# Three raw-word buffers instead of two, and one throw-away buffer instead of two, in a fused attention and mixer kernel

## The chip, the cores and the metric

One core of one Trainium2 chip runs the kernel. The metric is the device time of one execution in microseconds; of several executions the median counts. TensorE is called PE here, VectorE DVE, ScalarE ACT, GpSimd POOL, and SyncE, which issues nearly all DMAs, SP.

## What is computed

Causal attention over 4 batches, 12 heads, 448 tokens and 64 columns a head; then a mixer block (token mixing 448 to 256 to 448, channel mixing 768 to 1536 to 768); then a second block with a rotation of its input. Cut to what matters:

```python
attn = softmax(where(causal, q @ k.T / 8, -1e9)); x = attn @ v      # (4, 448, 768)
h   = relu(x.T @ w_tok1) @ w_tok2;  u = x + h.T
x2  = u + relu(u @ w_ch1) @ w_ch2
th  = x2 @ w_theta
y   = w_tok_r @ (x2 * cos(th)) + w_tok_i @ (x2 * sin(th));  u2 = x2 + y
out = u2 + relu(u2 @ w_ch)
```

The weights come as 64-bit floats, so that each weight is two 32-bit words in memory, and the kernel makes its own numbers of them.

## The kernel before

**Stages.** The first stage does attention in 24 pairs of heads, seven tiles of scores a pair, so 168 steps (the loop over `steps`, lines 600 to 643). A step makes one tile of scores on PE, its mask and minimum on DVE (L338), its exponential on ACT (L340), and four steps later the product with v. Pairs 0 to 11 turn the exponentials on PE (L347); later pairs send them through a DMA transpose issued on SP (L363). Beside the steps, channel-mixing units of the first block (`ch1_unit`, `ch2_unit`, matmul lines 227 to 229) are strewn in from step 50 on; each needs a weight tile `ws` that SP loads back from memory (`stream_tile`, L222). After the steps come the rest of these units and the second block.

**The rounding pipeline.** Twenty-eight weight tiles are made during the first stage: tiles 0 to 3 are the token weights (512 or 448 columns), tiles 4 to 27 the channel weights (768 columns). `ROUNDINGS` gives each tile j its step `at_step`: 3, 4, 8, 9 and then 14, 17, 20, 24 and so on to 92. A tile goes through this chain:

- `fetch(j)` takes a `raw` buffer and loads the 64-bit words on SP (L170),
- `round_first(j)` at `at_step`: ACT reads the high words (`abs64`, L173) into a `wf` tile,
- `round_bits(j)` one step later: three DVE instructions (L180, L181, L182), of which the last two read `raw`; after L182 the buffer is free. For a channel tile, ACT then squares the tile into a throw-away tile `junk`, of which only the sum is used (`squares`, L124),
- `round_split(j)` and `round_store(j)` three and five steps later make two half-precision parts and store them (L536).

Two steps after `at_step` the next fetch is put in: before the change `fetch(j + 2)`, into the buffer that tile j has just left.

**Six late tiles** (the weight of the last matmul, `convert_late` and `convert`) use the same `raw` and `wf` buffers. Their fetches are tied behind the load of q of pair 16 on SP (`loads[16]`, line 543).

**What sets the order.** The kernel is written as one list; a planner that runs its own model of the chip (`schedule_with_timeline_sim=True`) puts the instructions of each engine into a fixed order, and places a buffer's next user by when the model sees the buffer free. At run time each engine, and SP's queue too, goes through its list in order: an instruction that waits holds up all that stands behind it.

Of the kernel before, what the change touches and what calls it, by code (L numbers as in the profile page):

```python
# [25 lines left out]
FH = 6  # L26
NEG = -1.0e30
PSC = 32768.0
BUFS = dict(ut=12, h2=8, acc=12, ws=8, wf=3, raw=2, sb=3, ph=3, pt=5, t=3, junk=2)
NATIVE = {0, 1, 2, 3, 4, 5, 6, 7}  # L30
NATPV = {0, 1, 2, 3, 4, 5, 6, 7, 8, 9, 10, 11}
AHEAD, LAG, LOOK = 500, 4, 2
# [22 lines left out]
def fused(ctx, tc, q, k, v, w_tok1, w_tok2, w_ch1, w_ch2, w_theta, w_tok, w_ch, out):  # L55
# [53 lines left out]
    def hl_tile(tag):  # L109
        return main.tile([P, 2, S], F16, tag=tag, name=tag, bufs=BUFS[tag])  # L110

# [8 lines left out]
    def squares(dst, src):  # L120

        j = main.tile([P, E], BF16, tag="junk", name="junk", bufs=BUFS["junk"])
        with nc.allow_low_precision(reason="it only chooses a power of two"):
# [25 lines left out]
    def acc_tile():  # L149
        return main.tile([P, S], F32, tag="acc", name="acc", bufs=BUFS["acc"])  # L150

# [14 lines left out]
    def raw_tile():  # L166
        return cv.tile([P, E, 2], U32, tag="raw", name="raw", bufs=BUFS["raw"])

    def fetch64(src, raw):
        nc.sync.dma_start(out=raw[:, :src.shape[-1]].rearrange("p n w -> p (n w)"), in_=src.bitcast(U32))  # L170
# [13 lines left out]
    def wf_tile():  # L184
        return main.tile([P, E], F32, tag="wf", name="wf", bufs=BUFS["wf"])

# [23 lines left out]
    def ws_tile():  # L210
        return main.tile([P, 2, E], F16, tag="ws", name="ws", bufs=BUFS["ws"])

# [34 lines left out]
    for j in range(BUFS["sb"]):  # L247
        sb = ac.tile([P, 512], F32, tag=f"sb{j}", name=f"sb{j}")
# [4 lines left out]
    def tok_weights(n):  # L253
        if n < 2:
            cols = slice(n * 512, (n + 1) * 512)
            return w_tok1[:, cols], wt1[:, :, cols]
        return w_tok2[:, (n - 2) * S:(n - 1) * S], wt2[:, n - 2]
# [177 lines left out]
    h2 = {}  # L435
# [51 lines left out]
    def load_unit(n):  # L487
        if n < len(units) and n not in loaded and (n >= 24 or n in stored):
            b, fh, c, t = units[n]
            loaded[n] = stream_tile(wd[f"c{c}", fh, t])  # L490
# [4 lines left out]
    def split_ready():  # L495

        b = halves[0]
        if b < B and None not in accs[b]:
            s = s_u[:, b:b + 1]
            power(p_u[:, b:b + 1], s, sq_u[b])  # L500
            for d in range(DT):
                uTs[b][d] = hl_tile("ut")
                split_to(pick("uhi"), uTs[b][d], accs[b][d], s)
            halves[0] += 1

    def fetch(j):
        if j < len(ROUNDINGS):
            n = ROUNDINGS[j][1]
            src = tok_weights(n + 4)[0] if n < 0 else jobs[n][0]
            fetched[j] = src, raw_tile()  # L510
            fetch64(*fetched[j])

    def round_first(j):
        src, raw = fetched[j]
        rounding[j] = wf_tile()[:, 0:src.shape[-1]]
        abs64(rounding[j], raw)

    def round_bits(j):
        n, f = ROUNDINGS[j][1], rounding[j]
        round64(f, fetched.pop(j)[1])  # L520
        if n < 0:
            split_w(tok_weights(n + 4)[1], rounding.pop(j))
        else:
            rounding[j] = f, row_squares(f)

    def round_split(j):
        n = ROUNDINGS[j][1]
        if n >= 0:
            f, sq = rounding.pop(j)
            rounding[j] = ws_tile()  # L530
            split_scaled("P", rounding[j], f, jobs[n][2], sq)

    def round_store(j):
        n = ROUNDINGS[j][1]
        if n >= 0:
            nc.sync.dma_start(out=jobs[n][1], in_=rounding.pop(j))  # L536
            stored.add(n)
# [3 lines left out]
    def convert_late(n):  # L541
        while made[0] < min(n, len(late)):
            with tc.issue_after(loads[min(LATE_CONVERT, max(loads))].ins):
                convert(*late[made[0]])
            made[0] += 1
# [4 lines left out]
    def run_units(n):  # L550
        for _ in range(n):
            u = at[0]
            load_unit(u)
            b, fh, c, t = units[u]
            if c == 1 and t == 0:
                h_scale[0] = domain(b, fh)
            if c == 1:
                ch1_unit(b, uTs[b], fh, t, loaded[u])
            else:
                ch2_unit(b, uTs[b], accs[b], fh, t, loaded[u])  # L560
            loaded[u] = None
            at[0] += 1
            for ahead in range(LOOK + (u >= 24)):
                load_unit(at[0] + ahead)
            if at[0] % 24 == 2 and 1 <= at[0] // 24 <= 3:
                x_scale(at[0] // 24 - 1)
# [16 lines left out]
    def late_step(n):  # L583
        b, pr, t = steps[n]
        pp = pairs[b, pr]
        pv(pp, *TILES[t])
        if mixes:
            with tc.issue_after(pp.pv.ins):
                mix_tokens()
        if t == 6:  # L590
            if pr % 2 == 0:
                xgs[b, pr // 2] = [ap2.tile([P, 4, 2 * P], F32R, tag=f"xg{z}", name=f"xg{z}", bufs=1) for z in range(2)]
            finish(pp, xbufs[pr % 2], xgs[b, pr // 2])
            if pr % 2 == 1:
                mixes.append((b, pr // 2))

    def queued(pp):
        return tc.issue_after(pp.sent.ins) if pp.sent is not None else ExitStack()

    for n, (b, pr, t) in enumerate(steps):  # L600
        if t == 0:
            eng.update(ENGINES.get(b * NPR + pr, {}))
        if t == 0:
            pairs[b, pr] = Pair(b, pr, parts[b, pr])
        with tc.high_priority(AHEAD):
            scores(pairs[b, pr], *TILES[t])
        if n == 0:
            fetch(0)
            fetch(1)
        for j, (at_step, _) in enumerate(ROUNDINGS):  # L610
            if at_step == n - ROUND_BITS:
                with tc.issue_after(pairs[b, pr].first.ins):
                    round_bits(j)
            if at_step == n:
                with tc.issue_after(pairs[b, pr].last.ins):
                    round_first(j)
            if at_step == n - ROUND_FETCH:
                with queued(pairs[b, pr]):
                    fetch(j + 2)
            if at_step == n - ROUND_STORE:  # L620
                with queued(pairs[b, pr]):
                    round_store(j)
        if n >= 140:
            convert_late((n - 136) // 4)
        if t == 0 and (b, pr) != (B - 1, NPR - 1):
            nx = (b + (pr + 1) // NPR, (pr + 1) % NPR)
            with tc.high_priority(AHEAD), ExitStack() as es:
                if nx == (0, 1):
                    es.enter_context(tc.issue_after(loads[0].ins))
                parts[nx] = prep(*nx)  # L630
        if n >= LAG:
            with tc.high_priority(AHEAD):
                late_step(n - LAG)
            with tc.issue_after(pairs[steps[n - LAG][0:2]].pv.ins):
                for j, (at_step, _) in enumerate(ROUNDINGS):
                    if at_step == n - ROUND_SPLIT:
                        round_split(j)
                if n in (b2 * 42 + 48 for b2 in range(B)):
                    split_ready()
        if n == FIRST_UNIT - 4:  # L640
            load_unit(0)
            load_unit(1)
        run_units(sum(at_step == n for at_step in UNIT_STEPS))
# [169 lines left out]
    for b in range(B):  # L813
        raw, x2 = raws[b], x2s[b]
# [138 lines left out]
```

## Time and profile before

| | us |
|---|---|
| median of 3 runs | 913.49 (911.87 to 916.33) |
| the profiled execution, its own time | 915.05 |
| its span, first to last instruction | 913.3 |
| PE busy in the span | 871.4 (95%) |
| DVE busy | 630.5 (69%) |
| ACT busy | 537.2 (59%) |
| mean granted clock of PE | 0.98 of full speed |

The rows further down come from that one execution. Times in them are microseconds from the start of the span. A busy PE isn't PE at its peak, since matmuls are pipelined; what is read here are the stretches in which PE is idle, what ended them, and the granted clock in and after them.

### The profile page before, as it was taken

How to read it: one execution, taken by the hardware profiler on the slowest of the kernel's cores; microseconds unless marked ns; L12 is line 12 of the kernel's file. 1: busy time of each engine (PE TensorE's matmuls, PEld its weight loads, DVE VectorE, ACT ScalarE, POOL GpSimd, SP SyncE). 2: the span in 40 equal slices, each digit the busy share in tenths (PEclk: the TensorE clock that was granted, in tenths of full speed). 3: DMA queues.
4: the chain of work that ended last, by engine and by line, in shares of the span. 5: the costliest groups of instructions: out<-in, count | busy, mean ns of one | idle time of the engine just before them, and what ended most of it. 6: DMA issues, size and time to landing. Idle time of an engine off the chain costs nothing.

```text
span 913.3 us, 16742 instructions
## 1 busy us (share of the span) xinstructions
PE 871.4 (95%) x5979; PEld 566.4 (62%) x5979; DVE 630.5 (69%) x1499; ACT 537.2 (59%) x1247; POOL 169.6 (19%) x313
## 2 busy tenths in 40 slices
PE   7899899998879989999999999999999999999998
PEld 6778767776746656666665664556545556555554
DVE  6888897969998564748686337867875556666442
ACT  6777786767656553627574328546755456566441
POOL 2233243314121010011201103152111001001000
PEclk9999999999889989999999999999999999999999
DMA  6665776757699974849467469740450231331011
GB/s 174 205 207 170 278 245 222 265 192 213 165 284 290 292 169 120 193 140 204 120 181 219 142 186 299 277 140 10 135 151 18 96 113 37 94 113 35 23 63 71
DMA packets 105795, 149.67 MB, mean 164 GB/s; under 512 B 61104, under 2 KB 72304, under 8 KB 105712
## 3 DMA queue, kind: packets, MB, share of 16 engines
q1 hardware_dynamic: 105168, 147.59, 54.4%
q0 software_dynamic: 384, 0.79, 0.4%
q8 instruction: 47, 0.77, 0.4%
q14 instruction: 36, 0.29, 0.1%
q10 hardware_dynamic: 160, 0.23, 0.1%
HBM read 112.39 MB, written 22.81 MB: 148 GB/s over the span
## 4 chain that ended last, share of the span: by engine, by line
PE 73%; DMA 13%; DVE 7%; ACT 4%; issue 2%; SPq 1%; POOL 0%; ACTq 0%; DVEq 0%; POOLq 0%
PE ps_mm L227 16%; PE ps_mm L228 16%; PE ps_mm L229 16%; DMA pt<-ph 6%; PE ps_pv L375 3%; PE ps_sc L227 3%; PE ps_sc L331 3%; PE ps_sc L228 3%; PE ps_sc L229 3%; DMA ws<-w_c 2%; DMA raw<-in_w_ch_dram 2%; PE ps_pv L386 2%; PE ps_mm L347 2%; PE ps_sc L333 1%; DMA rawt<-x2d 1%
## 5 line engine op out<-in xcount | busy, mean ns | idle before, releaser
L227 PE MATMUL ps_mm<-h,ws 128*128 128x448 f16 x432 | 152.6, 354 | 1.1 <-DMA ws<-w_c 0.6
L228 PE MATMUL ps_mm<-h,ws 128*128 128x448 f16 x432 | 152.8, 354 | 0.0
L229 PE MATMUL ps_mm<-h,ws 128*128 128x448 f16 x432 | 152.6, 354 | 0.0
L227 PEld LDWEIGHTS <-ws 128*128 128x128 f16 x720 | 70.8, 98 | 69.0 <-issue 5.6
L229 PEld LDWEIGHTS <-ws 128*128 128x128 f16 x720 | 70.8, 98 | 64.5 <-issue 4.2
L228 PEld LDWEIGHTS <-ws 128*128 128x128 f16 x720 | 70.8, 98 | 61.6 <-issue 4.4
L340 ACT ACTIVATE sb<-sb,mx 128x320 f32<-128x320 f32 (+3 forms) x168 | 89.3, 532 | 32.0 <-DVE mx L338 30.8
L227 PE MATMUL ps_mm<-ut,ws 128*128 128x448 f16 x288 | 102.4, 357 | 5.5 <-DMA ws<-w_c 3.7
L228 PE MATMUL ps_mm<-ut,ws 128*128 128x448 f16 x288 | 102.8, 357 | 0.4 <-DVE ut L193 0.3
L229 PE MATMUL ps_mm<-ut,ws 128*128 128x448 f16 x288 | 102.7, 357 | 0.0
L338 DVE CUSTOM_DVE_ANT_0 sb<-ps_sc,mask 128x320 f32<-128x320 f32 (+3 forms) x168 | 74.3, 454 | 16.5 <-PE ps_mm L347 13.3
L124 ACT ACTIVATE junk<-acc 128x448 bf16<-128x448 f32 x72 | 41.1, 571 | 60.7 <-DVE acc L845 42.8
L375 PE MATMUL ps_pv<-v_raw,ptf 128*128 128x128 f32 (+1 forms) x456 | 65.9, 284 | 0.6 <-ACT sb L340 0.4
L375 PEld LDWEIGHTS ps_pv<-v_raw,ptf 128*128 128x128 f32 x456 | 61.7, 200 | 5.6 <-issue 1.9
L160 POOL TENSOR_SCALAR h<-t 128x448 f16<-128x448 f32 x48 | 33.1, 692 | 144.6 <-ACT t L459 144.3
L360 DVE SCALAR_TENSOR_TENSOR ph<-sb,ph 128x64 f16<-128x64 f32 (+3 forms) x156 | 44.3, 327 | 22.0 <-ACT ph L157 21.6
L459 ACT ACTIVATE t<-ps_mm,c_scale 128x448 f32<-128x448 f32 x48 | 29.9, 625 | 49.9 <-PE ps_mm L229 41.4
L157 ACT ACTIVATE ph<-sb 128x192 f16<-128x192 f32 (+3 forms) x84 | 36.0, 441 | 37.4 <-DMA pt<-ph 36.8
L461 DVE TENSOR_TENSOR h<-t,h 128x448 f16<-128x448 f32 x48 | 31.0, 649 | 32.3 <-POOL h L160 32.2
L130 POOL TENSOR_SCALAR f<-p_w,c_h 128x1 f32<-128x1 f32 x48 | 22.9, 479 | 145.1 <-DVE acc L473 129.0
L331 PE MATMUL ps_sc<-kh,qs 128*128 128x256 f32 (+2 forms) x112 | 44.6, 407 | 4.4 <-DVE g L140 2.3
L331 PE MATMUL ps_sc<-k_pad,q_raw 128*128 128x192 f32 (+3 forms) x112 | 41.1, 467 | 8.0 <-DMA k_pad<-in_k_dram 4.4
(210 smaller groups left out, 2115.4 us busy)
## 6 DMA issues: line engine op xcount, KB each, us to landing
ws<-w_c SPq DMA_DIRECT2D x120, 384.0 KB, 4.2
raw<-in_w_ch_dram SPq DMA_DIRECT2D x30, 768.0 KB, 4.6
w_c<-ws SPq DMA_DIRECT2D x30, 384.0 KB, 3.4
q_raw<-in_q_dram SPq DMA_DIRECT2D x16, 448.0 KB, 3.9
k_raw<-in_k_dram SPq DMA_DIRECT2D x16, 448.0 KB, 5.1
v_raw<-in_v_dram SPq DMA_DIRECT2D x24, 288.0 KB, 3.6
x2d<-acc SPq DMA_DIRECT2D x24, 224.0 KB, 2.9
acc<-x2d SPq DMA_DIRECT2D x24, 224.0 KB, 2.9
```

Source lines behind the costliest of these rows:

```text
L124: nc.scalar.activation(j[:, 0:src.shape[-1]], src, AF.Square, accum_out=dst)
L157: nc.scalar.activation(dst, src, AF.Copy, scale=scale)
L160: e.tensor_scalar(out=dst, in0=src, scalar1=scale, scalar2=0.0, op0=ALU.mult, op1=ALU.add)
L227: nc.tensor.matmul(ps, lhsT=ka(a[:, 0]), rhs=kb(b[:, 0]), start=first, stop=False)
L228: nc.tensor.matmul(ps, lhsT=ka(a[:, 0]), rhs=kb(b[:, 1]), start=False, stop=False)
L229: return nc.tensor.matmul(ps, lhsT=ka(a[:, 1]), rhs=kb(b[:, 0]), start=False, stop=last)
L331: nc.tensor.matmul(ps[:, 0:n], lhsT=lhs, rhs=cut(pp.kh), start=True, stop=pp.kl is None)
L338: pp.first = nc.vector.tensor_tensor_reduce(out=dst, in0=src, in1=msk, op0=ALU.add, op1=ALU.min, scale=-0.125, scalar=3.0e38, accum_out=pp ...
L340: pp.last = nc.scalar.activation(sb[:, 0:kk], sb[:, 0:kk], AF.Exp, bias=pp.mx[:, j:j + 1], scale=-1.0, accum_out=pp.sm[:, j:j + 1])
L360: nc.vector.scalar_tensor_tensor(out=dst, in0=sb[:, c0:c1], scalar=PSC, in1=hi[:, c0:c1], op0=ALU.mult, op1=ALU.subtract)
L375: pp.pv = nc.tensor.matmul(pp.ps[:, reg:reg + n], lhsT=pt[:, u], rhs=pp.v[0][:, vt * D:vt * D + n], start=(u == 0), stop=(u == len(blks) - 1))
L461: gates[0] = nc.vector.tensor_tensor(out=t[:, 1], in0=f, in1=t[:, 0], op=ALU.subtract)
```

## The change

The `raw` tag gets three buffers instead of two (6 KiB more in each partition: 768 columns of two 4-byte words), the `junk` tag one instead of two (1.5 KiB less: 768 columns of 2 bytes). The three places where a fetch is put in follow the buffer count: three fetches at the first step instead of two, and later `fetch(j + 3)` where `fetch(j + 2)` stood. Nothing else is touched.

```diff
-BUFS = dict(ut=12, h2=8, acc=12, ws=8, wf=3, raw=2, sb=3, ph=3, pt=5, t=3, junk=2)
+BUFS = dict(ut=12, h2=8, acc=12, ws=8, wf=3, raw=3, sb=3, ph=3, pt=5, t=3, junk=1)
@@ -605,8 +605,8 @@
         if n == 0:
-            fetch(0)
-            fetch(1)
+            for j in range(BUFS["raw"]):
+                fetch(j)
@@ -616,7 +616,7 @@
             if at_step == n - ROUND_FETCH:
                 with queued(pairs[b, pr]):
-                    fetch(j + 2)
+                    fetch(j + BUFS["raw"])
```

## Rows read from the trace of the kernel before

**Rows 1.** Windows by stage: stretch, length, busy us (instructions) per engine, PE clock, DMA, GB/s.

```profile
0.00:120.00 120.00, 106.91 (x697) 91.17 (x698) 94.66 (x264) 88.44 (x239) 39.31 (x67) 0.96 0.65 208
120.00:220.00 100.00, 99.50 (x686) 76.09 (x686) 84.50 (x201) 72.68 (x177) 31.62 (x42) 1.00 0.66 228
220.00:340.00 120.00, 103.10 (x895) 69.51 (x894) 98.32 (x262) 73.92 (x185) 19.79 (x36) 0.90 0.92 237
...
540.00:914.00 374.00, 365.66 (x2104) 204.13 (x2102) 231.56 (x454) 205.26 (x410) 53.81 (x112) 1.00 0.33 107
```

**Rows 2.** ACT's timeline: start, us, line, operation, and in brackets the idle before it.

```profile
17.54 0.62 ACT L173 ACTIVATE wf<-raw 128x448 f32<-128x448 f32 x1 [1.07 <-DMA raw<-in_w_tok_dram]
...
28.98 0.89 ACT L173 ACTIVATE wf<-raw 128x768 f32<-128x768 f32 x1 [2.21 <-DMA raw<-in_w_ch_dram]
...
64.68 0.90 ACT L173 ACTIVATE wf<-raw 128x768 f32<-128x768 f32 x1 [2.46 <-DMA raw<-in_w_ch_dram]
...
95.70 0.90 ACT L173 ACTIVATE wf<-raw 128x768 f32<-128x768 f32 x1 [2.20 <-DMA raw<-in_w_ch_dram]
```

**Rows 3.** PE's timeline: the matmuls that ended PE's idle time beside those four.

```profile
19.73 1.02 PE L331 MATMUL ps_sc<-k_pad,q_raw 128*128 128x448 f32 x2 [1.03 <-DVE mx L338]
...
30.79 1.86 PE L331 MATMUL ps_sc<-k_pad,q_raw 128*128 128x448 f32 x2 [2.13 <-DVE mx L338]
...
66.18 0.55 PE L347 MATMUL ps_mm<-ident,sb 128*128 128x128 f32 x3 [1.49 <-ACT sb L340]
...
97.20 0.55 PE L347 MATMUL ps_mm<-ident,sb 128*128 128x128 f32 x3 [1.34 <-ACT sb L340]
```

**Rows 4.** Windows of PE alone: stretch, length, busy us, clock, DMA share, GB/s.

```profile
30.00:36.00 6.00, 5.21 (x24) 0.72 0.39 124
68.00:72.00 4.00, 4.00 (x22) 0.57 0.77 230
98.00:104.00 6.00, 5.71 (x36) 0.72 0.63 236
...
256.00:264.00 8.00, 4.25 (x16) 0.57 1.12 259
```

**Rows 5.** SP's timeline: when DMAs were issued (a row may join two).

```profile
11.79 0.47 SPq L277 DMA_DIRECT2D k_pad<-in_k_dram  x1
...
13.42 3.62 SPq L170 DMA_DIRECT2D raw<-in_w_tok_dram  x2
...
22.25 0.33 SPq L170 DMA_DIRECT2D raw<-in_w_ch_dram  x1
...
59.48 0.33 SPq L170 DMA_DIRECT2D raw<-in_w_ch_dram  x1
```

**Rows 6.** DVE's timeline: the last reader of raw tile 1 and of raw tile 6.

```profile
15.94 0.68 DVE L182 SCALAR_TENSOR_TENSOR wf<-raw,wf 128x512 uint32<-128x512 uint32 x1
...
44.82 0.95 DVE L182 SCALAR_TENSOR_TENSOR wf<-raw,wf 128x768 uint32<-128x768 uint32 x1
```

**Rows 7.** A DMA issue on the page: count, KB each, median us from issue to landing.

```profile
ws<-w_c SPq DMA_DIRECT2D x120, 384.0 KB, 4.2
```

**Rows 8.** SP's own waits: for whom, us in total, times, longest us.

```profile
SPq L170 <- DVE wf L182: 67.9, 24, 6.7
```

**Rows 9.** SP's timeline: first and last fetches of the six late tiles.

```profile
248.38 1.47 SPq L170 DMA_DIRECT2D raw<-in_w_ch_dram  x2
...
456.15 0.33 SPq L170 DMA_DIRECT2D raw<-in_w_ch_dram  x1
```

**Rows 10.** The chain that ended last, at the weight tile behind the late fetches.

```profile
250.37 9.64 DMA ws<-w_c
```

**Rows 11.** PE's timeline: the matmul that waited for that weight tile.

```profile
260.06 0.55 PE L227 MATMUL ps_mm<-ut,ws 128*128 128x448 f16 x1 [3.75 <-DMA ws<-w_c]
```

**Rows 12.** The view of tile junk: the sum's read-out (ns min/median/max), longest idle before writers.

```profile
L124 ACT ACTIVATION_READ_ACCUMULATOR junk<-acc x72: 187/189/203, 50.4 to 883.0; 128x1 bf16 x72
...
  DVE acc L845: 42.8, 19
```

## The prediction

> **What bounds the kernel now.** I read the windows by stage first [rows 1]. From 540 us on PE is busy for 365.66 of 374 us (the rest is mostly the end), and from 120 to 220 us for 99.50 of 100, both at clock 1.00: there PE sets the pace and no buffer of raw words buys anything. PE is idle in two stretches: 13.1 us of the first 120 us (120 - 106.91), at clock 0.96, and 16.9 us from 220 to 340 us, at clock 0.90. Raw words are fetched in both, so I looked at each for itself.
>
> In the first stretch ACT's timeline shows four instructions that waited for a raw tile to land, 1.07 + 2.21 + 2.46 + 2.20 = 7.94 us [rows 2]; there are no others of any length among the 34 tiles. All four are the first reader, L173. ACT takes its list in order, so exponentials that were ready stood behind that wait, and PE ran dry beside each of them: 1.03 + 2.13 + 1.49 + 1.34 = 5.99 us idle [rows 3]. The reader is to see two things there: PE isn't waiting for the weights (no matmul of that stretch needs them yet), and what ended the idle time is named as ACT's L340 or DVE's L338, which themselves stood behind L173. After the second, third and fourth of these gaps the granted clock is at its lower level (1.2 instead of 2.4 GHz) for some microseconds; averaged over the rows' windows it is 0.72, 0.57 and 0.72 [rows 4]. What PE lost by that is its busy time times what was missing: 5.21 x 0.28 + 4.00 x 0.43 + 5.71 x 0.28 = 1.46 + 1.72 + 1.60 = 4.78 us. The gap at 19.73 us shows no such fall.
>
> **The third buffer, tiles 0 to 27.** A fetch can't start before the buffer it wants has been read for the last time, which is L182. With two buffers, the fetch of tile 4 left at 22.25 us and that of tile 9 at 59.48 us [rows 5]; each left as tile j - 2 was done, and landed when ACT was already waiting. With three it waits for tile j - 3: for tile 4 that is tile 1, done at 15.94 + 0.68 = 16.62 us, for tile 9 it is tile 6, done at 44.82 + 0.95 = 45.77 us [rows 6]. So they can leave 5.6 and 13.7 us earlier, against ACT waits of 2.21 and 2.46 us. Tile 2, which left at 13.42 us [rows 5], is fetched at the start and has about eight microseconds more, against 1.07 us; tile 13 is like tile 9. All four waits are covered, the tightest with 5.6 - 2.2 = 3.4 us to spare. What goes: the idle time, 5.99 us, and the slow clock behind it, 4.78 us, together 10.8 us. The low end is the idle time alone, 6.0 us, if PE's clock falls anyway because other small gaps stand nearby. I take 10.8, since the three windows of slow clock follow right behind three of the gaps and end within some microseconds. Whether the saving lasts to the end of the kernel: what follows is a stage in which PE has no room [rows 1], so a head start there is kept, and all later work is tied to steps and not to a time.
>
> **What the earlier fetches move past.** On SP the fetch still stands two steps behind its tile's start and still waits for the same L182; what is in the transfer is another tile. So the time that SP stands still for this (67.9 us in 24 waits [rows 8]) and what waits behind it, the loads of q, k and v, stay as they are: no cost. One transfer is new at its place: tile 2 (448 KB) at the start, behind tiles 0 and 1. The next DMA in SP's queue left at 11.79 us [rows 5]. If the new transfer were still running then, it would cost at most about the landing time of a load of its size, 4.2 us [rows 7], on the load of pair 2, which has no reader at once; I take zero and keep no more than that in the range. The last place, where tile 27 was fetched, falls empty.
>
> **The late tiles.** The six late tiles share the buffers. Their fetches are tied behind q of pair 16, and right behind it two of them left at 248.38 us, both buffers being free; the last went only at 456.15 us [rows 9]. The weight tile `ws` that was issued next took 9.64 us to land [rows 10], where 4.2 us are usual [rows 7], and PE stood idle for 3.75 us until it came [rows 11], with 2.25 us of another gap just before. So the two late tiles ahead of it cost that load 9.64 - 4.2 = 5.4 us, 2.7 us each. With three buffers free, a third late fetch will most likely go at the same place: another 2.7 us, and PE waits for all of it, since it had nothing else in its order. The ends are 0 (the third comes behind `ws`) and 2.7 us; below nothing too, a gain of 2.7 us, if the planner puts one late fetch less ahead of `ws` than now. I take 2.7. The last late fetch no longer goes at 456 us, where nobody waited for it: nothing.
>
> The Trainium skill, DMA: Bandwidth & Descriptors, sections "Queues, rings and completion order" and "Issuing engines are not separate DMA queues", speaks against this part of the change: a ring's descriptors are taken in the order in which they were put in, and all issuers share the same 16 DMA engines, so a deep prefetch holds up whatever is behind it. By that rule, carried to its end, every further raw tile ahead of a load that somebody waits for costs its whole transfer. The trace agrees at this one place (9.64 against 4.2 us); it does not in the first 105 us, where no load beside the raw tiles was waited for once the first scores had begun. Its result as a whole is the slower rival below.
>
> **One throw-away buffer.** Every `junk` tile is written by ACT alone and read by nobody. With two buffers already every third square overwrote the first one's tile, so all but two of 115 show what a reuse costs: the longest idle time before them was for DVE's `acc` [rows 12], and none was for ACT itself. Zero. If the planner did put a wait between two squares, it would be for the sum's read-out, 0.19 us each [rows 12], which ACT at 59% busy hides, and of which only the dozen and a half in the first 105 us could reach PE: under 3.4 us, and only if each fell on a full list.
>
> **The sum.** -10.8 + 2.7 = -8.1 us. From the profiled execution, 915.05 us (span 913.3 and 1.75 around it), that is 907.0. This execution lay 1.56 us above the median of the three runs, so against the median, 913.49, it is 905.4 us.
>
> **The rivals.**
>
> *The clock falls anyway, or other small waits move in.* Then only the idle time goes: -6.0 + 2.7 = -3.3, 910.2 us. For it: in the same 120 us ACT and DVE are busy 88.44 and 94.66 us [rows 1], so they have not much room. Against it: PE resumed 0.6 to 1.6 us after each of the four L173 had ended [rows 2, 3]. 15%.
>
> *The fetches don't come earlier.* The planner may leave a fetch on SP behind a load or store that itself waits, so that it lands when it did; the time stays at 913.5, or 916.2 with the late tile's 2.7. Against it: 5.6 and 13.7 us is a lot of room to lose. 10%.
>
> *The late tiles clog the DMAs: slower.* From 220 to 340 us the DMA engines are 0.92 busy [rows 1]. The sixth late tile comes into that stage instead of at 456 us, and each bunch of late fetches goes ahead of weight tiles and transposes that PE waits for. The price of one such gap as the trace has it is 2.25 + 3.75 us idle and 4.25 x 0.43 = 1.83 us of slow clock [rows 4, 11], 7.8 us. If the two bunches (three fetches each) each cost one gap more than now, 15.6 us, and the front gives its low end, the sum is +9.6, 923.1 us. It begins to decide where the extra gaps exceed 10.8 us. For it: the 9.64 us landing. Against it: between 260 and 340 us most late fetches ran with no PE wait behind them. 10%.
>
> *The late fetches leave their place.* The order of all engines is planned anew; if `ws` then comes ahead of one raw tile more than now, the time is 913.5 - 10.8 - 2.7 = 900.0 us. 7%.
>
> **How the numbers follow.** The forecast has 58% and its own range is 902.7 (front gain whole, no late cost) to 910.2 us. The range to hold 8 in 10 takes in the rivals on either side but the slower one: 900.0 to 915.0 us. About 0.5%, 4.6 us, is what a measurement of this kernel can tell from no change. Faster by more: 58 + 7 = 65%. Within: 15 + 10 = 25%. Slower: 10%.
>
> **What would show it.** Right: no ACT wait for a raw tile at L173 in the first 110 us; PE idle in the first 120 us down from 13.1 to about 7 us and its clock there up from 0.96 to near 1.00; the turn into the next stage some 10 us earlier; three fetches in a row behind q of pair 16 and the `ws` behind them landing in 11 to 13 us. Wrong: the four waits gone but PE's idle time in the first 120 us unchanged (then ACT's wait wasn't the last one), or PE's idle time from 220 to 340 us grown by more than 5 us, or a squaring on ACT that waits for ACT.

## The result and the profile after

The changed kernel takes 905.74 us (median of 5 runs, 904.31 to 907.62) against 915.07 for the kernel before beside it (911.87 to 916.33): a ratio of 0.9903 [0.9877, 0.9929], some 9 us, where 8.1 were forecast. The execution profiled after took 907.62 us, with a span of 905.8 (913.3 before).

Windows by stage of the kernel after; columns and the lines of before are those of [rows 1]:

```profile
0.00:120.00 120.00, 104.34 (x705) 87.88 (x706) 104.69 (x276) 94.90 (x252) 37.03 (x68) 0.96 0.74 241
...
220.00:340.00 120.00, 109.72 (x940) 74.17 (x938) 99.15 (x267) 74.11 (x184) 24.96 (x36) 0.93 0.92 251
```

The first stage is a surprise: PE is idle for 15.7 us of the first 120 (13.1 before) at the same clock, 0.96, though this is where the change was to act. The stage from 220 us has what is missing: PE idle 10.3 us from 220 to 340 us instead of 16.9.

The waits for raw tiles are gone all the same. What ended ACT's idle time before L173 in the first 120 us, us and times; before, four raw tiles ended 7.94 us of it [rows 2]:

```profile
  DVE ws L193: 1.2, 2
  DMA raw<-in_w_tok_dram: 0.4, 1
```

SP's timeline after, fetches and what was issued around them ([rows 5, 9] answer to it):

```profile
4.33 1.38 SPq L170 DMA_DIRECT2D raw<-in_w_tok_dram  x3
...
16.71 0.33 SPq L170 DMA_DIRECT2D raw<-in_w_ch_dram  x1
...
40.55 0.33 SPq L170 DMA_DIRECT2D raw<-in_w_ch_dram  x1
...
240.80 0.37 SPq L279 DMA_DIRECT2D q_raw<-in_q_dram  x1
241.22 0.42 SPq L170 DMA_DIRECT2D raw<-in_w_ch_dram  x1
241.73 0.38 SPq L281 DMA_DIRECT2D k_raw<-in_k_dram  x1
242.17 0.93 SPq L170 DMA_DIRECT2D raw<-in_w_ch_dram  x2
244.87 1.67 SPq L363 DMA_TRANSPOSE pt<-ph  x1
246.59 0.58 SPq L222 DMA_DIRECT2D ws<-w_c  x1
...
295.47 0.60 SPq L170 DMA_DIRECT2D raw<-in_w_ch_dram  x1
```

Tile 4 leaves at 16.71 us (22.25 before; the prediction had 16.62) and tile 9 at 40.55 (59.48 before; 45.77 in the prediction, which left out that the front itself runs ahead).

Totals by the clock on the wall mix work that has moved, so the two traces were laid beside each other by step: when the mask of the same score tile (L338) starts. DVE's timeline, the 49th and the 55th score tile, before:

```profile
100.53 0.62 DVE L338 CUSTOM_DVE_ANT_0 sb<-ps_sc,mask 128x448 f32<-128x448 f32 x1
...
120.45 0.61 DVE L338 CUSTOM_DVE_ANT_0 sb<-ps_sc,mask 128x448 f32<-128x448 f32 x1
```

and after:

```profile
90.23 0.61 DVE L338 CUSTOM_DVE_ANT_0 sb<-ps_sc,mask 128x448 f32<-128x448 f32 x1
...
117.29 0.61 DVE L338 CUSTOM_DVE_ANT_0 sb<-ps_sc,mask 128x448 f32<-128x448 f32 x1
```

At step 48 the kernel after leads by 10.3 us, six steps later by 3.2. Worked out in the same way from one profiled execution of each kernel, in us against the kernel before (minus is earlier):

| kernel | raw, junk buffers | step 48 | 54 | 84 | 132 | 162 |
|---|---|---|---|---|---|---|
| before, start of the step | 2, 2 | 100.5 | 120.4 | 211.6 | 367.9 | 478.1 |
| after | 3, 1 | -10.3 | -3.2 | -1.2 | -10.9 | -8.0 |
| E1 | 3, 2 | -8.7 | -9.1 | -9.1 | -10.7 | -9.7 |
| E2 | 2, 1 | -6.2 | +1.3 | +3.7 | -5.3 | -4.7 |
| E3 | 3, 1 | -9.8 | -2.7 | -1.9 | -11.7 | -13.0 |
| E4 | 3, 1 | -9.3 | -2.1 | -1.1 | -11.6 | -13.9 |
| E5 | 3, 1 | -9.8 | -7.0 | -5.6 | -13.0 | -13.7 |
| E6 | 3, 2 | -8.8 | -9.8 | -9.8 | -13.3 | -10.1 |
| E7 | 3, 1 | -10.1 | -3.8 | -1.0 | -12.7 | -9.3 |
| E8 | 3, 2 | -7.5 | -8.0 | -7.4 | -15.5 | -14.0 |
| E9 | 2, 2 | -1.2 | -2.3 | -2.3 | -6.9 | -7.1 |
| E10 | 3, 2 | -7.6 | -8.2 | -7.5 | -9.6 | -11.3 |
| E11 | 2, 2 | -3.2 | -4.3 | -3.6 | -9.9 | -11.6 |

How far one execution stands for its kernel shows in pairs of kernels with nearly the same lists. On PE, ACT, DVE, POOL and SP, E9 has the lists of the kernel before up to 249 us, and yet leads by 2.3 us at step 84. E3 has those of the kernel after but for the place of one fetch at about 212 us, and is 5.0 us away from it at step 162. Differences up to that size can't be told from chance, in the front and behind it.

So in the kernel after the lead is won before step 48, all but lost until step 84 (-10.3 to -1.2, that is 9.1 us), and found again by step 132. What it is won by shows in PE alone from the start to step 48, of the kernel before, the kernel after and E2, which has two raw buffers:

```profile
0.00:100.53 100.53, 88.82 (x572) 0.96 0.64 198
0.00:90.23 90.23, 83.34 (x577) 1.00 0.72 224
0.00:94.30 94.30, 84.03 (x577) 1.00 0.67 207
```

From before to after, PE's idle time falls from 11.7 to 6.9 us, by 4.8, and the clock's part, 88.82 x 0.04 = 3.6 us, goes; together these are 8.4 of the 10.3 us.

Where it is lost: PE's timeline after, the matmuls that ended its longer idle times (in brackets the idle time and what ended it); the third row belongs to the late tiles:

```profile
108.06 0.91 PE L375 MATMUL ps_pv<-v_raw,ptf 128*128 128x64 f32 x6 [1.66 <-DVE x L398]
114.57 0.53 PE L227 MATMUL ps_mm<-ut,ws 128*128 128x448 f16 x1 [5.61 <-ACT ut L157]
...
253.98 0.23 PE L386 MATMUL ps_pv<-v_raw,pt 128*128 128x64 bf16 x1 [3.35 <-DMA pt<-ph]
```

and PE alone in windows behind that gap (stretch, length, busy us, clock, DMA share, GB/s):

```profile
114.00:117.00 3.00, 2.15 (x8) 0.50 0.94 327
117.00:120.00 3.00, 3.00 (x9) 0.50 0.87 344
120.00:123.00 3.00, 3.00 (x23) 0.89 0.02 8
```

That is 1.66 + 5.61 = 7.27 us idle, and 2.15 x 0.50 + 3.00 x 0.50 + 3.00 x 0.11 = 2.9 us of clock: 10.2 us in one place. The kernel before has no idle time over 0.7 us between steps 48 and 54. The matmul at 114.57 is the first of the first channel-mixing unit and needs `ut`, which ACT makes with the scale `s_u`. POOL makes that scale, among other small products (L130). POOL's timeline before:

```profile
115.53 0.19 POOL L130 TENSOR_SCALAR p_u<-g 128x1 f32<-128x1 f32 x1
115.68 0.99 POOL L130 TENSOR_SCALAR s_u<-g 128x1 f32<-128x1 f32 x1
116.77 0.27 POOL L130 TENSOR_SCALAR c_h<-p_fh,p_u 128x1 f32<-128x1 f32 x1
117.13 1.33 POOL L130 TENSOR_SCALAR f<-p_w,c_h 128x1 f32<-128x1 f32 x4
```

and after:

```profile
109.06 0.83 POOL L130 TENSOR_SCALAR p_u<-g 128x1 f32<-128x1 f32 x1 [5.38 <-DVE g L140]
109.99 1.17 POOL L130 TENSOR_SCALAR c_h<-p_fh,p_u 128x1 f32<-128x1 f32 x1
111.26 2.40 POOL L130 TENSOR_SCALAR f<-p_w,c_h 128x1 f32<-128x1 f32 x4
113.64 0.18 POOL L130 TENSOR_SCALAR s_u<-g 128x1 f32<-128x1 f32 x1
```

The order is another: `s_u`, for which ACT and PE wait, now stands behind `c_h` and four `f`, which the matmul at 114.57 does not need. Nothing in the diff names these instructions.

### The profile page after: what moved, and what is told of

It is laid out like the page before. It is cut to its first block, busy times and chain, and to the rows that moved or that the text cites. A ratio compares the mean times of both kernels' runs of the same rounds, so it can differ in the third digit from the quotient of the medians.

```text
span 905.8 us, 16756 instructions
## 1 busy us (share of the span) xinstructions
PE 868.4 (96%) x5979; PEld 563.7 (62%) x5979; DVE 632.0 (70%) x1499; ACT 538.1 (59%) x1247; POOL 166.0 (18%) x313
## 4 chain that ended last, share of the span: by engine, by line
PE 74%; DVE 10%; DMA 8%; ACT 3%; issue 3%; POOL 1%; SPq 1%; DVEq 0%; ACTq 0%; POOLq 0%
PE ps_mm L228 17%; PE ps_mm L227 17%; PE ps_mm L229 17%; DMA pt<-ph 4%; PE ps_sc L229 3%; PE ps_sc L227 3%; PE ps_sc L228 3%; PE ps_pv L375 3%; PE ps_sc L331 2%; PE ps_pv L386 2%; PE ps_mm L347 2%; DVE sb L338 1%; PE ps_sc L333 1%; DVE wf L181 1%; DMA ws<-w_c 1%
## 5 line engine op out<-in xcount | busy, mean ns | idle before, releaser
L338 DVE CUSTOM_DVE_ANT_0 sb<-ps_sc,mask 128x320 f32<-128x320 f32 (+3 forms) x168 | 73.8, 454 | 13.2 <-PE ps_mm L347 8.8
L375 PE MATMUL ps_pv<-v_raw,ptf 128*128 128x128 f32 (+1 forms) x456 | 63.2, 276 | 1.9 <-DVE x L398 1.7
L375 PEld LDWEIGHTS ps_pv<-v_raw,ptf 128*128 128x128 f32 x456 | 58.8, 191 | 6.9 <-ACT sb L340 1.9
L130 POOL TENSOR_SCALAR f<-p_w,c_h 128x1 f32<-128x1 f32 x48 | 24.6, 516 | 145.2 <-DVE acc L473 129.0
L473 DVE SCALAR_TENSOR_TENSOR acc<-ps_mm,f,acc 128x448 f32<-128x448 f32 x48 | 32.4, 678 | 25.1 <-PE ps_mm L229 24.9
L227 PE MATMUL ps_sc<-th,ut 128*128 128x384 f16 x144 | 46.9, 326 | 0.0
```

The lines of the kernel that those rows point to most:

```text
L227: nc.tensor.matmul(ps, lhsT=ka(a[:, 0]), rhs=kb(b[:, 0]), start=first, stop=False)
L338: pp.first = nc.vector.tensor_tensor_reduce(out=dst, in0=src, in1=msk, op0=ALU.add, op1=ALU.min, scale=-0.125, scalar=3.0e38, accum_out=pp ...
L375: pp.pv = nc.tensor.matmul(pp.ps[:, reg:reg + n], lhsT=pt[:, u], rhs=pp.v[0][:, vt * D:vt * D + n], start=(u == 0), stop=(u == len(blks) - 1))
L473: nc.vector.scalar_tensor_tensor(out=acc[d], in0=ps[:, 0:S], scalar=f, in1=acc[d], op0=ALU.mult, op1=ALU.add)
```

## The experiments

Each was timed in 5 rounds against the kernel before on its own chip: 913.95 us there for E1 to E4 (23 runs), 913.83 for E5 to E8 (14), 914.43 for E9 to E11 (17). The edits of E1 to E8 are against the kernel after, or as stated.

**E1: three raw buffers, two throw-away buffers.**

```diff
-raw=3, ... junk=1
+raw=3, ... junk=2
```

> The raw edit alone: three raw buffers, three fetches ahead, still two throw-away buffers. If the third raw buffer makes the gain: no ACT wait for raw words in the first 110 us, the step-48 scores some 10 us earlier than before, and 904 to 908 us. If the time comes from the new order that the planner happens to lay out after 200 us: the front is the same, but the end lies anywhere between 902 and 915 us, away from 905.7 by more than 2 us.

905.07 us, 0.9894 [0.9854, 0.9933]. The room of the second throw-away buffer wasn't needed: the kernel fits with both. The first window of E1:

```profile
0.00:120.00 120.00, 111.06 (x752) 92.11 (x753) 103.78 (x280) 96.03 (x257) 39.75 (x68) 1.00 0.74 236
```

This is the profile that was forecast for the change: PE idle 8.9 us (120 - 111.06), clock 1.00, the lead kept from step 48 (8.7) to step 84 (9.1). POOL makes `s_u` right behind `p_u`, as before, and PE has no long gap there. So with the raw buffers alone the front's gain is there and stays, and what takes it back in the kernel after comes with the throw-away buffer. The total doesn't show it: E1 can't be told from the kernel after.

**E2: one throw-away buffer alone**, with the two raw buffers and the fetches of before. Against the kernel before:

```diff
-raw=2, ... junk=2
+raw=2, ... junk=1
```

> The throw-away edit alone: one junk buffer, two raw buffers. If junk costs nothing and brings nothing: 913 to 916 us, the four ACT waits for raw words (7.9 us) and PE's idle time from 220 to 340 us (16.9 us) as before. If what moved the late part is the planner's order, and one buffer less is enough to change that order: more than 3 us away from before on either side, with the four waits still there.

912.19 us, 0.9972 [0.9944, 0.9999]. PE's timeline of E2 at the first unit:

```profile
118.33 0.53 PE L227 MATMUL ps_mm<-ut,ws 128*128 128x448 f16 x1 [4.83 <-ACT ut L157]
```

The same gap without the third raw buffer, and the same loss: from -6.2 to +3.7, that is 9.9 us between steps 48 and 84 (9.1 in the kernel after). With E1 this is shown from both sides, and it holds in all thirteen kernels: between steps 48 and 54 the six with one throw-away buffer have an idle time of 2.5 to 5.6 us at the first unit, and the seven with two have none over 0.7 us anywhere there. E2 also has more lead at step 48 than it should have: ACT's waits for channel tiles fell from three to two (4.1 us) in its new order, and PE's clock did not fall before step 48 (1.00 against 0.96), though ACT still waits for raw tiles. From 211 to 368 us it wins 9.0 us back, and so ends near no change, 1.8 us below the kernel before, outside both of the ranges that were expected. PE is idle for 12.0 us from 220 to 340 us, not for 16.9 as expected.

**E3: three raw buffers, but the calls of the fetches as before.**

```diff
-            for j in range(BUFS["raw"]):
+            for j in range(2):
...
-                    fetch(j + BUFS["raw"])
+                    fetch(j + 2)
```

> Three raw buffers and one junk buffer, but the fetch calls stand where they stood: two at the first step and then tile j + 2. If the number of buffers decides when a fetch leaves and the place of the call doesn't: like the changed kernel, 904 to 908 us, no ACT wait for raw words in the first 110 us. If the call has to stand three tiles ahead: the four waits come back and the time is 912 to 916 us.

905.26 us, 0.991 [0.9883, 0.9937], with no wait for a raw tile and the leads of the kernel after up to step 132. SP's order differs from that of the kernel after in one fetch's place only. The buffer count moves the fetches; where they are called in the list does next to nothing.

**E4: the scales and `ut` of each batch (`split_ready`) made with priority**, to take the gap away.

```diff
-                    split_ready()
+                    with tc.high_priority(AHEAD):
+                        split_ready()
```

> The changed kernel with the making of the first matmul operands of each batch (split_ready) put at the same high priority as attention, so that its short chain over PE, DVE, POOL and ACT is not queued behind rounding work. If the 5.6 us for which PE waits for ut at 109 us is where the gain of the front was given back: that gap shrinks below 2 us, and the time is 899 to 903 us. If what is saved there is lost again before 220 us: the gap goes but the time stays at 904 to 908 us.

903.35 us, 0.9878 [0.9839, 0.9917]. A miss: the gap stayed at 5.29 us and POOL's order as it was (`s_u` at 114.69 us, behind `c_h` and `f`). The time can't be told from that of the kernel after.

**E5: on POOL, `s` before `p`, written out as an order.**

```diff
-        product(s, g[:, 1:2], 2.0 ** -51, 1.0)
-        product(p, g[:, 0:1], 2.0 ** 64, 1.0)
+        with tc.issue_after(product(s, g[:, 1:2], 2.0 ** -51, 1.0).ins):
+            product(p, g[:, 0:1], 2.0 ** 64, 1.0)
```

> The changed kernel, and every power computation makes its scale s before its counterpart p on POOL. In the changed kernel s_u starts at 113.64 us on POOL, behind c_h and four f (3.6 us), though its input was ready on DVE at 111.29. If that order is a part of what makes PE wait 5.6 us for ut: the gap at about 109 us shrinks by 2.3 us to about 3.3 us, and the time to 903 to 904 us. If the rest of the chain on DVE sets it: the gap stays above 5 us and the time at 905 to 907 us.

901.45 us, 0.9864 [0.9841, 0.9887], the lowest median of all, with E8 (the interval of the kernel after, [0.9877, 0.9929], overlaps it a little). POOL's timeline of E5:

```profile
110.44 0.19 POOL L130 TENSOR_SCALAR s_u<-g 128x1 f32<-128x1 f32 x1 [6.30 <-DVE g L140]
110.59 1.03 POOL L130 TENSOR_SCALAR p_u<-g 128x1 f32<-128x1 f32 x1
111.72 0.77 POOL L130 TENSOR_SCALAR c_h<-p_fh,p_u 128x1 f32<-128x1 f32 x1
```

and PE's:

```profile
111.93 0.53 PE L227 MATMUL ps_mm<-ut,ws 128*128 128x448 f16 x1 [2.52 <-ACT ut L157]
```

The gap falls from 5.61 to 2.52 us and the loss between steps 48 and 84 from 9.1 to 4.2. So POOL's order is the cause of about half of the loss. The gap fell by 3.1 us where 2.3 were expected: the expectation took DVE's L127 at 111.14 us for the input of `s_u`, but that one is the next weight tile's, and its own was done at 109.90 (109.76 + 0.14).

The 2.5 us that are left end on ACT's `ut` too. They point at DVE's order. PE's sum for `s_u` (L138) and DVE's last step behind it (L127), in the kernel after:

```profile
106.22 0.18 PE L138 MATMUL ps_mm<-sq_u,ones 128*128 128x1 bf16 x1
109.76 0.14 DVE L127 TENSOR_SCALAR g<-g 128x1 uint32<-128x1 uint32 x1
```

and in E1:

```profile
104.85 0.16 PE L138 MATMUL ps_mm<-sq_u,ones 128*128 128x1 bf16 x1 [0.22 <-ACT junk L124]
106.07 0.15 DVE L127 TENSOR_SCALAR g<-g 128x1 uint32<-128x1 uint32 x1
```

That is 3.4 us from the sum's end to DVE's step in the kernel after (3.1 in E5) and 1.1 in E1: with one throw-away buffer DVE has rounding work (L180, L181, L182) and other work ahead of it. No run changed this order by itself, so this half is read from the traces and not shown.

**E6 and E7: the late tiles' fetches tied to one pair each** instead of all to pair 16, in E1 and in the kernel after.

```diff
-            with tc.issue_after(loads[min(LATE_CONVERT, max(loads))].ins):
+            with tc.issue_after(loads[min(LATE_CONVERT + made[0], max(loads))].ins):
```

> Three raw and two junk buffers, and the late tiles' fetches tied one by one behind q of pairs 16, 17, 18 and so on instead of all behind pair 16. Without that edit, three late fetches left between 237.1 and 239.4 us, the transpose behind them took 9.72 us, and PE stood idle for 3.9 us until it came. If the bunch of late fetches is the cause: that transpose lands in 4 to 6 us, the gap of 3.9 us shrinks below 1.5 us, and the time is 901 to 903 us. If the transposes are late for another reason: a gap of 3 to 4 us stays there and the time is 904 to 906 us.

> The changed kernel (three raw, one junk) with the same edit of the late tiles: one fetch behind q of each of the pairs 16, 17, 18 and so on. In the changed kernel three late fetches left between 241.2 and 242.5 us and PE waited 3.4 us for a transpose behind them. If the bunch is the cause: the gap at 250.6 us goes and the time is 902 to 904 us. If not: the gap stays and the time is 905 to 907 us.

E6: 902.9 us, 0.9873 [0.9842, 0.9903]; E7: 907.72 us, 0.9933 [0.9909, 0.9956]; neither can be told from its parent. E1 has three late fetches between 237 and 239.4 us and then a gap of 3.87 us for a transpose. In E6 only one late fetch stands there and the transpose behind it lands in 6.79 us instead of 9.72, but PE's timeline still shows

```profile
246.02 0.23 PE L386 MATMUL ps_pv<-v_raw,pt 128*128 128x64 bf16 x1 [3.84 <-DMA pt<-ph]
```

since PE, in another order, ran out of other work 3.7 us sooner. In E7 the transpose lands in 4.98 us instead of 9.07 and the gap of 3.35 us is gone, and the time is no better. So the bunch does make the transposes late, by 1.5 us (E6) and 2.0 us (E7) a fetch, but the time doesn't follow from it.

**E8: E1 with the edits of E5 and of E6**, both as shown above.

> Three raw and two junk buffers, s before p on POOL, and late fetches spread. With two junk buffers there was no gap at the first unit, so s first should bring nothing there by itself; the time is that of the spread alone, 901 to 904 us, if the gaps are what they seem. If the planner's order decides more than these edits, it lies off by more than 3 us from the spread alone.

901.46 us, 0.9861 [0.9834, 0.9888]: like E5.

**E9: the kernel before with the edit of E6**, the late fetches spread.

> The kernel before, with the late tiles' fetches tied one by one behind q of pairs 16, 17, 18 and so on. SP's order is that of before up to q of pair 16, and from there one raw fetch less stands ahead of the weight tile ws that landed in 9.64 us. If a raw tile ahead of it costs that load 2.7 us: it lands in about 7 us, PE's gap of 3.75 us before 260 us shrinks to about 1 us, and the time is about 911 us. If the raw tiles aren't what makes it late: it still takes 9 us or more and the gap stays above 3 us.

906.56 us, 0.9919 [0.9888, 0.9951]. SP's order is that of before up to the load of q of pair 16; then one raw tile instead of two stands ahead of `ws`. The chain that ended last, and PE's timeline, of E9:

```profile
247.47 8.00 DMA ws<-w_c
```

```profile
255.51 0.56 PE L227 MATMUL ps_mm<-ut,ws 128*128 128x448 f16 x1 [1.95 <-DMA ws<-w_c]
```

Against 9.64 and 3.75 us [rows 10, 11], a late tile ahead of that load costs 1.6 to 1.8 us, not 2.7. But this gap isn't what moved the time by 8 us, where some 3 were expected: the waits for raw tiles are still there (6.7 us in three waits for channel tiles), the lead is 1 to 2 us up to step 84, where the lists are still those of before, and most of the rest comes later, in an order that was planned anew.

**E10: E1 with the edit of E5.**

> Three raw and two junk buffers with s before p in every power computation. With two junk buffers s_u already stood ahead of c_h and f on POOL and no gap stood at the first unit. If s first brings its gain only through that gap: the time is that of three raw and two junk buffers, 904 to 906 us. If it also helps in later batches: 900 to 903 us, with less PE idle time after 200 us.

903.48 us, 0.9879 [0.9835, 0.9922]: not to be told from E1 (905.07), as there was no gap there to close.

**E11: the kernel before with the edit of E5**, two raw buffers and two throw-away buffers.

> The kernel before (two raw, two junk buffers) with s before p in every power computation. If s first acts only where s_u stood behind other products: no change, 912 to 916 us, the four ACT waits for raw words as before. If it helps in later batches by itself: 908 to 911 us.

904.21 us, 0.9891 [0.985, 0.9933], faster than either range expected, with waits for raw tiles still in it: 1.0 us for a token tile, and for channel tiles, before L173 in the first 120 us (us, times):

```profile
  DMA raw<-in_w_ch_dram: 3.3, 2
```

Its lead is 3.2 us at step 48, 3.6 at step 84 and 9.9 at step 132. E9 and E11 together are a warning: small edits that leave the raw buffers alone gain as much in total as the change does (7.9 and 10.2 us), and in both most of the lead arises after step 84, where the planner laid out the stage from 220 to 340 us anew. By the time alone, the gain of the change couldn't be put down to its buffer. The step table can do that for the front.

## Why the prediction was right, and where it wasn't

The time (905.4 forecast, 905.74 measured) and the side were right. The steps held less well: two errors cancelled, so that the total came out within a microsecond is in part luck. By the step table the profiled executions give -10.3 us up to step 48, +9.1 from there to step 84, -9.7 to step 132 and +2.9 to step 162.

*The third buffer, -10.8 us: the mechanism right, the size only beside this one kernel before.* The fetch of tile 4 left when it was said to (16.71 against 16.62 us), none of the channel tiles 4 to 27 is waited for in any of the nine kernels with three raw buffers (late tiles are, in E6, E7 and E8, where their fetches were moved), and these lead by 7.5 to 10.3 us at step 48. The four with two buffers, the kernel before among them, lead by 0 to 6.2. Of the two terms, the idle time measures 4.8 us (5.99 forecast) and the clock 3.6 (4.78). The clock's term is the weaker one: the two-buffer kernels still wait for raw tiles, and up to step 48 their clock is 0.96 (before), 0.98 (E9, with the same lists), 1.00 (E2) and 1.00 (E11). And E2 leads by 6.2 us already, so with one throw-away buffer the third raw buffer adds 4.1 us there. E1 shows the forecast's own signs, clock 1.00 and PE's idle time of 8.9 us (about 7 were named). The rival in which the clock falls anyway is refuted by that for the front, and the one in which the fetches don't come earlier by SP's rows.

*One throw-away buffer, zero: wrong where it acts, and this is the step of the working that failed.* As argued, no square waits for another one: in the kernel after, the view of `junk` names only DVE ahead of its writers. But the step looked for the price in the instructions that use the buffer. What changed was the order that the planner laid out for others: `s_u` behind five products on POOL, PE idle for 5.61 us and at clock 0.50 behind it. The loss from step 48 to 84 is 9.1 us with three raw buffers and 9.9 with two (E2), against 0.4 us gained in E1. The bound of "under 3.4 us" was therefore no bound at that place. On the total no price is shown: one throw-away buffer instead of two makes, by the ratios of 914 us, -2.6 us with two raw buffers (E2), +0.8 with three (the kernel after against E1), +5.5 with late fetches spread (E7 against E6) and -1.4 with `s` first (E5 against E10); they have no common sign. Why the planner turned the order around for one buffer less wasn't found out.

*The sign "the four waits gone, but PE's idle time in the first 120 us unchanged"* did come (15.7 against 13.1 us), and the prediction would have read it wrongly, as ACT's wait not having been the last. A total over a stretch can't tell an old gap that stayed from a new one that came; the steps can.

*The late tiles, +2.7 us: mis-sized.* Three fetches do go at q of pair 16, with k of that pair between the first and the second. What stood behind them was a transpose, and PE waited for one for 3.35 us, where it had been idle for 3.75 + 2.25 us [rows 11]: at this place 2.6 us less instead of 2.7 more. The price of one late tile ahead of `ws` measures 1.6 to 1.8 us (E9), where 2.7 was taken. PE shows no wait for the weight tile behind them either: it was issued at 246.59 us and landed in 8.3 us, not in the 11 to 13 us of the forecast. The rule of the Trainium skill, DMA: Bandwidth & Descriptors, "Queues, rings and completion order", that descriptors are taken in ring order, agrees in its direction with E9 (8.00 against 9.64 us), but the slower rival built on it did not come: PE is idle 6.6 us less from 220 to 340 us, not 15.6 more.

*SP's order, zero:* nothing in the traces contradicts it; SP stands still for L182 for 72.2 us in 27 waits (67.9 in 24 before).

*"A head start is kept": not shown.* E1 keeps its lead of about 9 us from step 48 to step 162, so there it looks right. But the kernels with three raw buffers that had lost all but 1 to 2 us of it by step 84 (after, E3, E4, E7) stand at step 132 at 10.9 to 12.7 us, as do those that kept 7 to 10 (E1, E6, E8, E10: 9.6 to 15.5). What the kernel after found again is seen in PE's waits (us in total, times, longest) from 220 to 340 us. Before:

```profile
PE ps_pv L386 <- DMA pt<-ph: 6.5, 5, 2.7
PE ps_mm L227 <- DMA ws<-w_c: 4.4, 2, 3.7
PE ps_sc L331 <- DVE g L140: 2.3, 1, 2.3
PE ps_sc L331 <- DVE mx L338: 2.1, 3, 1.3
PE ps_pv L386 <- issue: 1.6, 1, 1.6
```

and after:

```profile
PE ps_pv L386 <- DMA pt<-ph: 3.8, 2, 3.4
PE ps_mm L227 <- DMA ws<-w_c: 2.8, 1, 2.8
PE ps_pv L386 <- issue: 2.0, 1, 2.0
PE ps_mm L412 <- DVE xg L164: 0.9, 1, 0.9
```

These are 16.9 us against 9.5 (some short waits of the kernel after left out; its idle time is 10.3 in all). Why this stage, in which the DMA engines are 0.92 busy, gives back to a late kernel what it had lost stays open: its own pace by the DMAs, an unlucky order in the kernel before, and the last late fetch going at 295 instead of 456 us would all look like this. E6, E7 and E9 moved those fetches and don't settle it. The second has most for it: from 220 to 340 us the kernel before has the most idle time and the lowest clock of all thirteen (16.9 us and 0.90; the others 9.8 to 13.9 us and 0.93 to 0.99), and from step 84 to 132 every other kernel gains on it, by 1.6 to 11.7 us. E2 gains 9.0 there with two raw buffers, so this part of the change's gain can't be put down to the third one.

What can be said of the total: with the third raw buffer it is 8.9 us lower where two throw-away buffers stay (E1) and, by the ratios of E2 and of the kernel after, about 6 us where there is one (0.9972 - 0.9903 = 0.0069 of 914). That the buffer makes these is not shown, since E9 and E11 gain as much without it. Where the second throw-away buffer is given up, `s` put first on POOL (E5) is the order to try: it beats the kernel before clearly, and the kernel after by some 4 us, with intervals that overlap a little.

## What to carry to other kernels

In a kernel whose order is planned anew on every edit, lay the two traces beside each other by step before you put a gain or a loss down to a buffer: here, in one execution of each, a total that was right within a microsecond hid 10 us won, 9 lost and 10 found again. Take two executions of one order beside them, to see how far two traces differ by themselves (2.3 us at step 84 here). A scratch buffer that nobody waits for can still cost at one place, because with one buffer less the planner places other engines' instructions differently; undo such a part by itself (E1) before paying with it for room. And where a short chain of small products releases the next stage, write out the order that makes the awaited one first (E5: 5.61 us of idle time down to 2.52).

## What the runs showed of the hardware

PE's clock lies at its lower level right behind the new gap: 0.50 from 114 to 120 us after 5.61 us without a matmul, 0.89 in the next three. In E5, after 2.52 us, it does so too, though it comes back sooner. PE alone in E5:

```profile
112.00:114.00 2.00, 2.00 (x8) 0.50 1.04 342
114.00:117.00 3.00, 3.00 (x17) 0.91 0.83 291
```

So what the clock takes on top was 2.9 us behind the gap of 5.61 us and 2.00 x 0.50 + 3.00 x 0.09 = 1.3 us behind that of 2.52.

The spans of POOL's products of 128x1 aren't fixed: the same `s_u` shows 0.18 us in the kernel after and 0.99 before, and four `f` show 2.40 and 1.33 us. Spans on POOL are rough, and no run shows what decides them.
